# Strassen's scheme in the second layer of a mixture of experts: seven products of quarters for eight

## The chip, the cores and the metric

The kernel runs on one core of a Trainium2 chip. The metric is the device time of one execution in microseconds. Verdicts compare runs of two kernels made on the same chip in the same rounds. Each run has a state; unless one is named as slow below, all runs here are fast ones. The clock below is the one granted to TensorE, as a share of full speed.

## The reference

Attention without a softmax makes 4608 tokens of 512 features. Then a gate gives each token to one of eight experts, in the order of the logits, until each expert has exactly 576. An expert is a two-layer perceptron, all in float32:

```python
N, D, E, F = (4608, 512, 8, 1024)
cap = N // E                                  # 576 tokens per expert
order = np.argsort(-(x @ w_gate).flatten())
for idx in order:                             # greedy, balanced
    tok, e = (int(idx) // E, int(idx) % E)
    if assigned[tok] >= 0 or counts[e] >= cap:
        continue
    assigned[tok] = e
    counts[e] += 1
for e in range(E):
    mask = assigned == e
    h = np.maximum(x[mask] @ w1[e], 0.0)      # 576x512 @ 512x1024
    out[mask] = h @ w2[e]                     # 576x1024 @ 1024x512
```

## The kernel before

The greedy order is not walked. The kernel settles one expert after another, and finds the tokens of each by a search for a threshold. While TensorE computes expert t, the search for the tokens of expert t+1 runs between its matmuls. One step of the search is a round trip: TensorE counts how many tokens lie over each of 32 candidate thresholds (nine small matmuls into `n_ps`), VectorE works out the next candidates in a dozen tiny instructions and one large comparison (`over`), and TensorE loads `over` for the next count.

```python
def compare(over, cand, c0=0, c1=GC):
    nc.vector.tensor_tensor(over[:, c0:c1], ...mx..., ...cand..., op=AL.is_ge)   # 128x1152, both in SBUF

def threshold(t, over):
    for s in range(NSTEP):
        yield (4.6 if t > 1 else 4.3) if s > 0 else ...    # us of matmuls before the next step
        for c in range(0, GC, G):
            nc.tensor.matmul(n_ps, lhsT=over[:, c:c + G]..., rhs=best[:, :, c:c + G], ...)
        # ... need, full, n_full from n_ps
            nc.vector.tensor_scalar(some, in0=n_full..., scalar1=0.5, ..., op0=AL.is_gt)
            nc.vector.transpose(some_t..., some...)
            nc.vector.reduce_sum(out=kk, in_=some_t, axis=AXX)
            nc.vector.tensor_scalar(from_lo, in0=kk, ...)
            for g in range(G):                              # G = 4
                nc.vector.tensor_scalar(ends[g * QP:(g + 1) * QP], in0=from_lo, scalar1=lo_was[0:QP], ...)
        if s + 1 < NSTEP:
            cand_next = candidates(s + 1, lo)
            compare(over, cand_next)
        # ... then assign(): cut, two, sums, ... with both inputs in SBUF
```

The numbers after `yield` are the only timing: a fixed order of TensorE's instructions, in which the next count stands 4.6 us of matmuls after the last. The second layer of an expert takes its 576 tokens as four whole blocks of 128 and a rest of 64:

```python
for n, (a, nr) in enumerate(blocks):
    if nr == P:                                             # a whole block: 8 matmuls of 512 columns
        for f in range(FC):
            nc.tensor.matmul(y_ps, lhsT=hid[:, f, a:a + nr], rhs=w2[:, f, :],
                             start=(f == 0), stop=(f == FC - 1))
            yield 0.858
        nc.scalar.copy(y_sb, y_ps)
    else:
        # ... the rest of 64 rows
    put(t, n, nr, y_sb)                                     # scatter from GpSimd
```

## Time and profile before

| | before |
|---|---|
| time, median of the first 3 runs | 726.95 us (724.67 to 729.97) |
| granted clock, whole run | 0.940 |
| expert stage, eight experts | 534.55 us of the span of 723.6 |
| TensorE idle in the expert stage | 0.87 us (534.55 - 533.68) |
| GpSimd busy in the expert stage | 77.78 us |

First the windows by expert of the kernel before, here the fourth expert, the last one, and the sum of all eight. After the length come the busy us (and instructions) of TensorE, its weight loads, VectorE, ScalarE and GpSimd, then the clock:

```profile
383.40:450.98 67.58, 67.46 (x302) 41.06 (x303) 46.21 (x167) 12.62 (x27) 10.74 (x10) 1.00 0.29 100
651.46:713.75 62.29, 62.24 (x208) 37.34 (x208) 0.68 (x1) 9.51 (x22) 4.80 (x5) 1.00 0.06 19
sum 534.55, PE 533.68 PEld 323.71 DVE 287.42 ACT 98.39 POOL 77.78; mean PE 66.71 PEld 40.46 DVE 35.93 ACT 12.30 POOL 9.72
```

TensorE has almost no idle time, at full clock. The last expert has no search beside it (VectorE is busy for 0.68 us). Second, two lines of the timeline in the middle of a search step, before. A line has the start and the length in us, the engine (PE is TensorE, PEld its weight loads, DVE VectorE, ACT ScalarE, POOL GpSimd), the line of the program (L729), the operation, what it writes and reads, the shapes and the count; a bracket at the end gives the idle time before it and what ended that:

```profile
399.88 5.10 PE L729 MATMUL h_ps<-xt,w_sb 128*128 128x288 f32 x20
401.83 0.92 DVE L500 TENSOR_SCALAR ends<-from_lo,ends 32x2 f32<-32x2 f32 x4
```

### The profile page before, as it was taken

The numbers are of one execution on the slowest core, as the hardware profiler recorded it, in microseconds if no ns is written. First come the engines' busy times: TensorE is split into PE (matmuls) and PEld (weight loads), VectorE is DVE, ScalarE is ACT, GpSimd is POOL, SyncE is SP. The second block draws the span as 40 slices with busy tenths as digits, with TensorE's granted clock in tenths as the row PEclk, the third lists the DMA queues.
The fourth block names the chain that finished last, engine by engine and source line by source line (L and its number), as shares of the span: only waits on it lengthen the run. The fifth ranks groups of instructions, "written<-read, shape, count | busy, mean of one in ns | idle before, by whom it ended". The sixth has DMA issues, their size and how long they took to land.

```text
span 723.6 us, 12335 instructions
## 1 busy us (share of the span) xinstructions
PE 641.3 (89%) x4979; PEld 408.7 (56%) x4979; DVE 395.6 (55%) x1382; ACT 164.5 (23%) x331; POOL 97.5 (13%) x113
## 2 busy tenths in 40 slices
PE   3877788116999999999999999999999999999994
PEld 3666666112764576457546744774576467447641
DVE  4344646888787378657766774887477530010000
ACT  1454555101210311122122202110221122122100
POOL 0100110003004100510041023004100421010011
PEclk9987977557999999999999999999999999999998
DMA  8987898305308200900260054008200944010001
GB/s 286 312 269 262 283 315 322 125 0 194 113 1 298 74 1 3 347 24 0 91 259 23 1 191 173 9 0 295 77 1 10 340 161 169 14 43 8 1 29 36
DMA packets 41400, 93.34 MB, mean 129 GB/s; under 512 B 3456, under 2 KB 3456, under 8 KB 41344
## 3 DMA queue, kind: packets, MB, share of 16 engines
q1 hardware_dynamic: 34752, 72.49, 28.8%
q0 software_dynamic: 5888, 20.06, 7.9%
q8 instruction: 39, 0.64, 0.3%
q14 instruction: 17, 0.14, 0.1%
q10 hardware_dynamic: 704, 0.02, 0.1%
HBM read 72.50 MB, written 20.05 MB: 128 GB/s over the span
## 4 chain that ended last, share of the span: by engine, by line
PE 64%; issue 19%; DVE 9%; DMA 2%; POOL 2%; ACT 2%; POOLq 0%; ACTq 0%; DVEq 0%; SPq 0%
PE y_ps L740 23%; PE h_ps L729 23%; PE o_ps L372 3%; PE qt_ps L303 3%; PE y_ps L750 3%; PE kv_ps L315 3%; DVE over L268 2%; PE t_ps L700 2%; PE n_ps L462 2%; POOL out_dram L709 1%; DMA gw<-in_moe_w_gate_dram 1%; DVE need L468 1%; POOL xg L632 1%; DMA w_sb<-in_moe_w_dram 1%; DVE ends L500 1%
## 5 line engine op out<-in xcount | busy, mean ns | idle before, releaser
L729 PE MATMUL h_ps<-xt,w_sb 128*128 128x288 f32 x1024 | 261.7, 410 | 0.8 <-ACT xt L703 0.8
L740 PE MATMUL y_ps<-w_sb,hid 128*128 128x512 f32 x512 | 227.6, 595 | 0.0
L729 PEld LDWEIGHTS h_ps<-xt,w_sb 128*128 128x128 f32 x1024 | 190.1, 190 | 54.9 <-issue 5.7
L740 PEld LDWEIGHTS y_ps<-w_sb,hid 128*128 128x128 f32 x512 | 94.2, 190 | 100.8 <-issue 100.0
L732 ACT ACTIVATE hid<-h_ps 128x288 f32<-128x288 f32 x128 | 52.6, 411 | 212.4 <-PE h_ps L729 212.4
L709 POOL DMA_INDIRECT out_dram<-y_sb,outs x40 | 44.0, 1101 | 421.1 <-ACT y_sb L745 392.6
L687 DVE TENSOR_TENSOR xs<-xg 128x512 f32<-128x512 f32 (+1 forms) x40 | 27.3, 689 | 75.6 <-PE t_ps L700 65.2
L268 DVE TENSOR_TENSOR over<-mx,cand 128x1152 bf16<-128x1152 f32 (+3 forms) x52 | 67.0, 1288 | 1.6
L757 DVE TENSOR_TENSOR y_sb<-y_ps,y_part 64x512 f32<-64x512 f32 x8 | 5.5, 683 | 105.2 <-ACT y_part L756 105.2
L745 ACT COPY y_sb<-y_ps 128x512 f32<-128x512 f32 x32 | 18.7, 584 | 161.8 <-PE y_ps L740 161.8
L632 POOL DMA_INDIRECT xg<-x_dram,ids x40 | 40.3, 1008 | 76.3 <-DMA w_sb<-in_moe_w_dram 35.9
L703 ACT ACTIVATE xt<-t_ps,g_col 128x512 f32<-128x512 f32 (+1 forms) x40 | 25.8, 645 | 93.5 <-PE t_ps L700 50.6
L462 PEld LDWEIGHTS <-over 128*128 128x128 bf16 x441 | 17.4, 97 | 38.6 <-DVE over L268 30.2
L372 PE MATMUL o_ps<-kvx,qt 64*64 64x72 f32 x1152 | 32.5, 257 | 7.3 <-issue 6.3
L462 PE MATMUL n_ps<-best,over 128*128 128x32 bf16 x441 | 19.4, 179 | 21.0 <-DVE over L268 18.6
L303 PE MATMUL qt_ps<-ident,q_sb 128*128 128x128 f32 x144 | 31.2, 345 | 5.5 <-ACT kvt L336 1.9
L315 PE MATMUL kv_ps<-v_sb,k_sb 64*64 64x64 f32 x1152 | 29.1, 246 | 7.3 <-issue 7.3
L380 DVE TENSOR_REDUCE ms<-sq 128x8 f32<-128x512 f32 x36 | 24.1, 680 | 19.2 <-ACT sq L378 19.0
L372 PEld LDWEIGHTS o_ps<-kvx,qt 64*64 64x64 f32 x1152 | 26.3, 158 | 13.5 <-issue 11.8
L500 DVE TENSOR_SCALAR ends<-from_lo,ends 32x2 f32<-32x2 f32 x144 | 31.6, 219 | 2.8
L700 PEld LDWEIGHTS t_ps<-ident,xs 128*128 128x128 f32 (+1 forms) x160 | 18.3, 140 | 24.3 <-issue 16.7
L315 PEld LDWEIGHTS kv_ps<-v_sb,k_sb 64*64 64x64 f32 x1152 | 26.1, 158 | 8.8 <-issue 8.8
(174 smaller groups left out, 479.0 us busy)
## 6 DMA issues: line engine op xcount, KB each, us to landing
w_sb<-in_moe_w_dram SPq DMA_DIRECT2D x16, 1024.0 KB, 6.2
w_sb<-in_moe_w_dram SPq DMA_DIRECT2D x8, 2048.0 KB, 16.4
k_sb<-in_k_dram SPq DMA_DIRECT2D x16, 576.0 KB, 5.7
v_sb<-in_v_dram SPq DMA_DIRECT2D x16, 576.0 KB, 5.8
q_sb<-in_q_dram SPq DMA_DIRECT2D x16, 576.0 KB, 5.7
x_dram<-o_sb SPq DMA_DIRECT2D x16, 576.0 KB, 4.4
x_dram<-o_sb SPq DMA_DIRECT2D x4, 288.0 KB, 3.4
xg<-x_dram,ids POOLq DMA_INDIRECT x40, 6.5
```

Source lines behind the costliest of these rows:

```text
L268: nc.vector.tensor_tensor(over[:, c0:c1], mx[:, c0:c1].rearrange("p (c o) -> p c o", o=1).to_broadcast([P, c1 - c0, NCAND]), cand[:, 1:NCA ...
L303: nc.tensor.transpose(t_ps[:, x, :], q_sb[:, (4 * n + x) * P:(4 * n + x + 1) * P], ident)
L315: nc.tensor.matmul(kv_ps[cs, l, r * D:(r + 1) * D], lhsT=k_sb[ls, r, j, :], rhs=v_sb[ls, r, j, :], start=(j < 2), stop=(j >= R - 2))
L372: nc.tensor.matmul(o_ps[n * HP:(n + 1) * HP, rp, (2 * r2 + l) * W:(2 * r2 + l + 1) * W], lhsT=turned_q[bn][ks, block // 2, l * HP:(l + 1) ...
L462: nc.tensor.matmul(n_ps, lhsT=over[:, c:c + G].rearrange("p c n -> p (c n)"), rhs=best[:, :, c:c + G], start=(c == 0), stop=(c == GC - G))
L500: nc.vector.tensor_scalar(ends[g * QP:(g + 1) * QP], in0=from_lo, scalar1=lo_was[0:QP], scalar2=None, op0=AL.add)
L632: tokens = nc.gpsimd.indirect_dma_start(out=xg[0:nr].rearrange("p h w -> p (h w)"), out_offset=None, in_=x_dram, in_offset=bass.IndirectOf ...
L700: nc.tensor.transpose(t_ps[:, d, 0:nr], xs[0:nr, d * P:(d + 1) * P], ident[0:nr, 0:nr])
L709: put = nc.gpsimd.indirect_dma_start(out=out, out_offset=bass.IndirectOffsetOnAxis(ap=ids_of[t][0:nr, n:n + 1], axis=0), in_=y_sb[0:nr, :] ...
L729: nc.tensor.matmul(h_ps, lhsT=w1[:, 2 * (d % 2) + d // 2, f * P:(f + 1) * P], rhs=xt[:, d, cs], start=(d == 0), stop=(d == DC - 1))
L732: nc.scalar.activation(hid[:, f, cs], h_ps, ACT.Relu)
L740: nc.tensor.matmul(y_ps, lhsT=hid[:, f, a:a + nr], rhs=w2[:, f, :], start=(f == 0), stop=(f == FC - 1))
```

## The change

Whole blocks hold 512 tokens, so the second layer's 512x1024 by 1024x512 product can be cut in quarters each way. Strassen's scheme (in Winograd's form) makes the result from seven products of quarters instead of eight, and pays with sums of operands before and sums of products after. One eighth of the whole-block second layer is saved on TensorE, which is the bound. The operand sums go to GpSimd, which has most of its time free; results are added on VectorE. Per expert there are on GpSimd four weight differences of 128x1024, eight token sums of 128x512 and one result difference of 128x512; VectorE gets six adds of 128x512.

```diff
+        tw = moe.tile([P, 4, FH, DH], FT, name="tw", tag="tw", bufs=1)
+        t1, t2, t3, t4 = (tw[:, n] for n in range(4))
+        for o, x, y in ((t1, b12, b11), (t2, b22, t1), (t3, b22, b12), (t4, t2, b21)):
+            in_order(nc.gpsimd.tensor_tensor(o, x, y, op=AL.subtract))
 ...
+        def sums(m):
+            ms = slice(m, m + 2)
+            for o, x, y, op in ((s1, a21, a22, AL.add), (s2, s1, a11, AL.subtract), (s3, a11, a21, AL.subtract),
+                                (s4, a12, s2, AL.subtract)):
+                in_order(nc.gpsimd.tensor_tensor(o[:, ms], x[:, ms], y[:, ms], op=op))
 ...
-                for f in range(FC):
-                    nc.tensor.matmul(y_ps, lhsT=hid[:, f, a:a + nr], rhs=w2[:, f, :], ...)
-                    yield 0.858
+        for m, (left, right, then) in enumerate(
+                ((a11, b11, lambda p_ps: nc.scalar.copy(u1, p_ps)), (a12, b21, first_c),
+                 (a22, t4, lambda p_ps: nc.scalar.copy(u5, p_ps)), (s2, t2, lambda p_ps: add(u2, p_ps, u1)),
+                 (s3, t3, seventh), (s1, t1, fifth), (s4, b22, third))):
+            p_ps = psm.tile([P, 2, DH], FT, name="y_ps", tag="y", bufs=3)
+            for n in range(2):
+                for f in range(FH):
+                    nc.tensor.matmul(p_ps[:, n], lhsT=left[:, f, n * P:(n + 1) * P], rhs=right[:, f], ...)
+                    yield 0.4
+            then(p_ps)
```

`in_order` fixes the order of GpSimd's queue. The change also moves the search: as soon as expert t+1's tokens are settled, the search for t+2 begins, still inside expert t, and its VectorE bursts are cut up by pauses. `xt` and `hid`, and in TensorE's result memory (PSUM) the transposes' `t_ps`, get one buffer in place of two to make room.

```diff
         ctl = control(t + 1) ...
+                    if wait is None:
+                        found = True
+                        if t + 2 < E - 1:
+                            ahead = control(t + 2)
+                            wait = next(ahead)
+                elif ahead is not None and used is not None:
+                    wait -= used
+                    if wait <= 0:
+                        wait = next(ahead)
```

## The prediction

The sum came to 727.0 - 25.5 + 11 = 712.5 us, put down as 712. The 11 us for the new wait were the author's guess, under a third of a worst case of 39 us. Rival (a) says that the GpSimd sums don't disturb VectorE, rival (b) that they hold up its search chain in each expert, for which the two stretched instructions spoke, and that the holes may also cost TensorE's clock, which is what its slices show.

> **What bounds the kernel now.** I read the page's busy shares and slices first, then the windows by expert, then the groups of instructions, then the timeline of one expert.
>
> ```profile
> PE 641.3 (89%) x4979; PEld 408.7 (56%) x4979; DVE 395.6 (55%) x1382; ACT 164.5 (23%) x331; POOL 97.5 (13%) x113
> PE   3877788116999999999999999999999999999994
> PEclk9987977557999999999999999999999999999998
> 322.10:389.70 67.60, 67.48 (x303) 41.08 (x303) 46.17 (x167) 12.62 (x26) 10.73 (x10) 1.00 0.28 100
> 592.50:657.00 64.50, 64.50 (x229) 39.30 (x228) 6.38 (x16) 12.62 (x26) 9.72 (x10) 1.00 0.26 93
> ```
>
> From slice 10 on (about 180 us) TensorE is full. The window rows give, after the length, busy us of PE, weight loads, VectorE, ScalarE and GpSimd, then the clock. One inner expert is 67.6 us long, PE has work for 67.48 of them at full clock, VectorE for 46, GpSimd for 11. So in the expert stage (179 to 714 us) every microsecond of matmul removed is a microsecond of time, unless something new makes PE wait.
>
> The last expert has no bookkeeping in it, so its matmuls run undisturbed:
>
> ```profile
> 651.34 31.31 PE L729 MATMUL h_ps<-xt,w_sb 128*128 128x288 f32 x128
> 682.49 27.63 PE L740 MATMUL y_ps<-w_sb,hid 128*128 128x512 f32 x64
> 710.05 3.65 PE L750 MATMUL y_ps<-w_sb,hid 128*64 128x512 f32 x16
> ```
>
> The kernel has 64 first-layer matmuls and 32 whole-block second-layer matmuls per expert, so each f32 matmul is two instructions. Taking off the last one's own length: (31.31 - 0.41)/127 = 0.2433 us per 288-column instruction, (27.63 - 0.59)/63 = 0.4292 us per 512-column one. That is 0.83 ns per column.
>
> Who else is close to setting the pace? The search for the next expert's tokens is a ping-pong between PE and VectorE, laid statically into PE's order:
>
> ```profile
> 400.07 0.15 DVE L468 TENSOR_TENSOR need<-goal,n_ps 32x8 f32<-32x8 f32 x1 [0.75 <-PE n_ps L462]
> ...
> 403.06 1.36 DVE L268 TENSOR_TENSOR over<-mx,cand 128x1152 bf16<-128x1152 f32 x1
> 404.34 0.15 DVE L511 TENSOR_TENSOR ends<-ends 128x1 f32<-128x1 f32 x1
> 404.58 0.52 PEld L462 LDWEIGHTS <-over 128*128 128x128 bf16 x9
> 404.82 0.38 PE L462 MATMUL n_ps<-best,over 128*128 128x32 bf16 x9
> ```
>
> VectorE starts a step at 400.07 and has `over` at 404.42; PE loads it at 404.58. The slack is some 0.2 us, in a step of 5.16 us. Anything that lengthens this chain by more than that stops PE, and PE has no spare time to make it up. This is the weak spot.
>
> [...] Weight loads take 190 ns, less than the 217 ns that a 256-column instruction will need, so I don't expect them to bind. [...] No GpSimd tensor_tensor is in this trace; its only large elementwise work is a one-input 64x512 copy of 0.61 us. [...]
>
> ```profile
> 369.06 1.36 DVE L268 TENSOR_TENSOR over<-mx,cand 128x1152 bf16<-128x1152 f32 x1
> 369.35 1.96 POOL L709 DMA_INDIRECT out_dram<-y_sb,outs  x1 [0.30 <-issue]
> 452.55 0.91 POOL L709 DMA_INDIRECT out_dram<-y_sb,outs  x1 [3.29 <-DVE need L468]
> 453.08 0.37 DVE L492 TENSOR_SCALAR some<-n_full 32x64 f32<-32x64 f32 x1
> ```
>
> The first scatter takes 1.96 us against a median of 0.98: about the time for which `over` still runs. The tiny `some`, normally 0.18 us, takes 0.37 and ends with the GpSimd instruction (453.45 against 453.46). Not every small VectorE instruction beside a GpSimd one is stretched, so the effect is real but its size for a GpSimd tensor_tensor is open.
>
> **The change part by part.**
> Products: 7 of 8 matmuls of 256 columns, 112 instructions, replace 64 of 512 columns. At 0.83 ns per column a 256-column one is 0.2433 - 32 x 0.00083 = 0.2168 us. 112 x 0.2168 = 24.3 us against 64 x 0.4292 = 27.5. Saved: 3.2 us per expert, times 8 = 25.5 us, all on the path. Transposes, search matmuls, first layer and the rest block of 64 rows stay.
> GpSimd: per expert four weight differences of 128x1024, 8 token sums of 128x512 and one result difference of 128x512. [...] Deadlines: the weight differences are first used in product 3, 38 us into the expert; the last sums begin at 31 us and the one used first (the second of four) is due at product 4, about 10 us later. Even behind five gathers (6.5 us) it is there. The first expert's w2 is there in time too: its load takes 16 us and starts with the layer.
> VectorE: six adds of PSUM and SBUF, 128x512. The trace has 0.69 us for such a size (xs), so 4.1 us; it goes from 46 to 50 of some 64 us. ScalarE copies two products in place of four blocks: less. [...] With three PSUM buffers for products of 3.5 us each, PE can run two products ahead of a late add.
> Moved: the search for expert t+2 now starts inside expert t, as soon as t+1's tokens are settled. Walking the generators, its steps still stand 10 first-layer matmuls (4.87 us) or 12 product matmuls (5.2 us) apart, so the slack of one step stays small; the whole search only drifts earlier, and by experts 6 and 7 is out of the way. Weights are fetched earlier, which is harmless. Single buffers for xt, hid and the sums: each is rewritten after its last reader in PE's order, so I see no new wait there.
> End: unchanged in kind, the rest block is still last (copy, add, scatter).
> Sum without new waits: 727.0 - 25.5 = 701.5 us.
>
> **The new wait.** The weight differences start about 2.6 us into an expert (the previous rest block's scatter ends there in the timeline). In experts 1 to 4 they fall on search steps, in expert 5 on the assignment. [...] The best is none. The kernel's many small pauses look like work of someone who timed this on the chip, and who would not have kept a 7 us hole in each expert; the step pause of 4.6 was left as it was. I therefore take about 11 us, under a third of the worst case: 701.5 + 11 = 712.5, which I round to 712.
>
> **The rivals.** (a) [...]the matmul saving comes through whole: 701 to 704. For it: PE is 100% full, the arithmetic is plain, GpSimd and VectorE both have room on average. Against: the scatter of 1.96 us and the 0.2 us of slack. (b) [...]720 to 740, the saving is given back. [...]the slices before 180 us, where PE waits, show 0.5 to 0.7. (c) VectorE's in-order queue: an add delayed behind a search burst holds a product's buffer. Near the end of an expert five scalings (3.4 us), four adds (2.8) and up to two search steps (8.7) fall into about 10 us, which is too much for VectorE; the buffers take some of it. Costs 1 to 2 us per expert, about 8 in all: 710. (d) Weight loads bind at 256 columns: with 0.24 in place of 0.217 us per instruction the saving would be nearly gone (112 x 0.24 = 26.9): about 722. Against: the load is shown as 190 ns and overlaps.
>
> **Range and chances.** 2% is 14.5 us, or 712.4: my centre sits on the border. (a) and (c) fall under or at it, (b) and (d) over it. Range 700 to 730. Faster by over 2%: 0.47. Within 2%: 0.42. Slower: 0.11[...].
>
> **What would show it.** PE's period in the products 0.217 us; the last expert shorter by 3.2 us (62.4 to 59.2) since no search runs in it: that tests the arithmetic alone. In experts 1 to 4: `over`, `ends` or `some` stretched beyond 1.36 and 0.22 us beside GpSimd tensor_tensors, and idle PE before n_ps released by `over`; the sum of these is my 11 us. Product matmuls waiting for a VectorE add would show (c). Wrong would be: an inner expert of 64.4 us with no idle (then 701), or one over 67.6 (then (b)).

## The result, and the profile after

| | before | after |
|---|---|---|
| median of 4 runs | 728.00 us (724.67 to 729.97) | 824.72 us (822.94 to 828.93) |
| granted clock, profiled run | 0.940 | 0.887 |
| sum of the eight experts, counted from 179.20 us | 534.55 us | 632.65 us |
| TensorE busy in them | 533.68 us | 543.51 us |
| TensorE idle in them | 0.87 us | 89.14 us |

The ratio is 1.134 (95% interval 1.128 to 1.141): the changed kernel is slower by 13%. A ratio here is the mean time of one kernel's fast runs over that of the other's fast runs of the same rounds, so it isn't quite the ratio of the medians. The four runs of the changed kernel are fast, and the four before lie within 0.8% of each other.

The page of the changed kernel, its busy shares and two rows of its slices (tenths, 40 slices):

```profile
PE 652.4 (79%) x5362; PEld 501.7 (61%) x5363; DVE 515.6 (63%) x1430; ACT 155.8 (19%) x315; POOL 263.6 (32%) x217
PE   4878871186897698958796988787987996999995
PEclk9978875588997899989898899978998997999998
```

TensorE was full from the eleventh slice on before. Now it has holes nearly everywhere in the expert stage, and its clock is below full in many slices. GpSimd is busy for a third of the span and VectorE for 63%, so by quantity neither is the bound. The windows by expert, for the same fourth expert, the last one and the sum:

```profile
436.52:521.51 84.99, 71.64 (x359) 54.37 (x360) 70.17 (x194) 11.56 (x25) 29.73 (x21) 0.91 0.22 75
752.85:811.85 59.00, 58.95 (x256) 46.45 (x256) 4.74 (x7) 8.34 (x20) 25.36 (x18) 1.00 0.05 18
sum 632.65, PE 543.51 PEld 415.36 DVE 405.38 ACT 89.80 POOL 243.78; mean PE 67.94 PEld 51.92 DVE 50.67 ACT 11.23 POOL 30.47
```

The last expert, with no search in it, got shorter: 62.29 to 59.00 us, 3.29 us saved, with no idle TensorE and full clock, although GpSimd's 25.36 us of work is all there. So the arithmetic works, and the operands are ready in time. The fourth expert, with a search in it, got longer by 17.41 us: TensorE is idle for 13.35 us (84.99 - 71.64) and its clock is 0.91.

What VectorE does meanwhile is the third thing to see: it is "busy" for 70.17 us in place of 46.21. About 4 of these are new adds and some belong to the search that now falls into this expert (without the sums, in the first experiment below, it is 55.97), but the last 14 us are no new work. An instruction that waits for the other engine counts as busy here (`some`, below, with 1.29 us for 0.18). The timeline of the changed kernel in that expert, in a search step from the count on:

```profile
440.93 2.36 POOL L746 TENSOR_TENSOR tw<-w_sb 128x1024 f32<-128x1024 f32 x1
...
442.05 1.29 DVE L492 TENSOR_SCALAR some<-n_full 32x64 f32<-32x64 f32 x1
443.36 2.35 POOL L746 TENSOR_TENSOR tw<-w_sb,tw 128x1024 f32<-128x1024 f32 x1
...
443.89 1.84 DVE L498 TENSOR_SCALAR from_lo<-kk,span 32x2 f32<-32x2 f32 x1
445.67 2.34 POOL L746 TENSOR_TENSOR tw<-w_sb 128x1024 f32<-128x1024 f32 x1
445.77 5.03 DVE L500 TENSOR_SCALAR ends<-from_lo,ends 32x2 f32<-32x2 f32 x4
447.97 2.34 POOL L746 TENSOR_TENSOR tw<-tw,w_sb 128x1024 f32<-128x1024 f32 x1
451.11 1.36 DVE L268 TENSOR_TENSOR over<-mx,cand 128x1152 bf16<-128x1152 f32 x1
452.53 0.42 PE L462 MATMUL n_ps<-best,over 128*128 128x32 bf16 x9 [6.34 <-DVE over L268]
```

Read it in pairs. `some` is issued while the first weight difference runs and ends at 443.34, when that difference has ended (443.29): 1.29 us for 0.18. The second difference starts at 443.36 and `from_lo`, issued at 443.89, ends when it ends: 1.84 us for 0.22. Then the four `ends`: 5.03 us for 0.92, across the third and fourth difference. VectorE gets its turn here about once per GpSimd instruction, and it can miss one: in the kernel with the sums alone (second experiment below) `some` took 2.81 us across a scatter and the first difference. `some_t` and `kk` between them, a transpose and a reduction, keep their lengths (0.23 and 0.21 us) beside the second difference. The step takes 11.67 us from count to count (440.86 to 452.53) where it took 5.17. TensorE has matmuls for 5.1 us of that, and the bracket of the last line says the rest: 6.34 us idle until `over` was there. The list of waits of the changed kernel, in the expert stage alone, sums such holes up (total us, times, longest):

```profile
PE n_ps L462 <- DVE over L268: 56.8, 14, 9.1
PE a_ps L617 <- DVE along L614: 12.3, 2, 7.1
PE all_ps L529 <- DVE sums_b L525: 10.5, 2, 8.0
PE t_ps L715 <- DVE xs L701: 9.3, 5, 2.7
```

Together they are 88.9 of the 89.14 us of idle time. `along` and `sums_b` belong to the assignment that follows a search, `xs` are the scaled tokens. The kernel before has no wait for `over` listed in this stage; its 18.6 us of them lie ahead of it.

### The profile page after: what moved, and what is told of

Same layout as the page of the kernel before. It is cut to its first block, busy times and chain, and to the rows that moved or that the text cites. A ratio compares the mean times of both kernels' runs of the same rounds, so it can differ in the third digit from the quotient of the medians.

```text
span 821.7 us, 13270 instructions
## 1 busy us (share of the span) xinstructions
PE 652.4 (79%) x5362; PEld 501.7 (61%) x5363; DVE 515.6 (63%) x1430; ACT 155.8 (19%) x315; POOL 263.6 (32%) x217
## 5 line engine op out<-in xcount | busy, mean ns | idle before, releaser
L765 PE MATMUL h_ps<-xt,w_sb 128*128 128x288 f32 x1024 | 280.4, 434 | 0.8 <-ACT xt L718 0.8
L756 POOL TENSOR_TENSOR sh<-hid 128x512 f32<-128x512 f32 x32 | 42.7, 1336 | 148.6 <-ACT hid L768 148.6
L814 PE MATMUL y_ps<-tw,sh 128*128 128x256 f32 x384 | 90.3, 390 | 0.0
L462 PE MATMUL n_ps<-best,over 128*128 128x32 bf16 x441 | 19.7, 181 | 77.2 <-DVE over L268 75.4
L814 PEld LDWEIGHTS y_ps<-tw,sh 128*128 128x128 f32 x384 | 73.3, 194 | 9.7
L785 DVE TENSOR_TENSOR y_sb<-y_ps,u 128x512 f32<-128x512 f32 x24 | 16.4, 684 | 92.2 <-PE y_ps L814 92.2
L500 DVE TENSOR_SCALAR ends<-from_lo,ends 32x2 f32<-32x2 f32 x144 | 63.9, 443 | 2.8
L814 PE MATMUL y_ps<-w_sb,hid 128*128 128x256 f32 x256 | 60.5, 392 | 0.0
L814 PEld LDWEIGHTS y_ps<-w_sb,hid 128*128 128x128 f32 x256 | 49.7, 196 | 7.4
L746 POOL TENSOR_TENSOR tw<-w_sb 128x1024 f32<-128x1024 f32 x16 | 37.6, 2351 | 12.2 <-DMA w_sb<-in_moe_w_dram 12.0
L814 PE MATMUL y_ps<-w_sb,sh 128*128 128x256 f32 x128 | 35.2, 410 | 0.0
```

What stands on the lines that cost most here:

```text
L462: nc.tensor.matmul(n_ps, lhsT=over[:, c:c + G].rearrange("p c n -> p (c n)"), rhs=best[:, :, c:c + G], start=(c == 0), stop=(c == GC - G))
L746: in_order(nc.gpsimd.tensor_tensor(o, x, y, op=AL.subtract))
L756: in_order(nc.gpsimd.tensor_tensor(o[:, ms], x[:, ms], y[:, ms], op=op))
L765: nc.tensor.matmul(h_ps, lhsT=w1[:, 2 * (d % 2) + d // 2, f * P:(f + 1) * P], rhs=xt[:, d, cs], start=(d == 0), stop=(d == DC - 1))
L814: nc.tensor.matmul(p_ps[:, n], lhsT=left[:, f, n * P:(n + 1) * P], rhs=right[:, f], start=(f == 0), stop=(f == FH - 1))
```

## The experiments

My theory after reading the trace: (T1) the operand sums on GpSimd hold up VectorE's search chain, instruction by instruction; TensorE idles, and its clock drops with the longer holes (it is 0.50 from 452.5 to 455 us, after the hole of 6.34 us above). This is theory L of the expectations. The rivals: (T2) the moved search or the split VectorE work stretch the chain by themselves; (T3) Strassen's products don't come through at full rate (weight loads, buffers, adds on VectorE).

### Both halves apart

The first experiment keeps everything of the change but the sums: the products read unsummed quarters (and give a wrong result).

```diff
-        for o, x, y in ((t1, b12, b11), (t2, b22, t1), (t3, b22, b12), (t4, t2, b21)):
-            in_order(nc.gpsimd.tensor_tensor(o, x, y, op=AL.subtract))
+        t1, t2, t3, t4 = b11, b22, b12, b21
+        s1, s2, s3, s4 = a21, a22, a11, a12
...
-            in_order(nc.gpsimd.tensor_tensor(quarter(1, 0), u3, u5, op=AL.subtract))
+            nc.scalar.copy(quarter(1, 0), u3)
```

> The changed kernel with all operand sums and the result difference on GpSimd taken out; the products read unsummed quarters, so the result is wrong on purpose. All else stays: seven products, six VectorE adds, the search moved ahead. Theory L [...]: nearly the whole loss goes, 702 to 715 us, clock in the expert stage back to 0.98 or more, `ends` back at 0.22 us. Rival V (VectorE's extra adds and the moved search overload it): the loss stays, 780 us or more. Rival N (256-column matmuls cost more than their columns): the last expert stays above 60 us.

Measured: 731.83 us (725.11 to 733.92), ratio 1.006 (0.999 to 1.014). Against the changed kernel's 1.134 the sums alone are worth 0.128 of about 727, or 93 us: most of the loss. But the time is not the 702 to 715 expected. The windows of this kernel, the fourth and the last expert:

```profile
399.42:468.58 69.16, 64.58 (x359) 50.36 (x360) 55.97 (x198) 12.18 (x26) 8.21 (x9) 1.00 0.27 94
663.25:722.25 59.00, 58.90 (x256) 46.41 (x256) 4.74 (x7) 8.95 (x21) 4.80 (x5) 1.00 0.05 18
```

TensorE has 64.58 us of work, 2.9 less than before, and the expert is 1.6 us longer all the same. The saving of 8 x 3.29 = 26.3 us is there and some 31 us are lost elsewhere (26.3 + 0.006 x 727). That is T2 or part of T3, and is taken up below.

The second experiment is the reverse: the kernel before, with its old second layer and its old search, and the same 13 GpSimd instructions per expert at the same places, whose results nobody reads (right result).

```diff
+        for o, x, y in ((t1, b12, b11), (t2, b22, t1), (t3, b22, b12), (t4, t2, b21)):
+            in_order(nc.gpsimd.tensor_tensor(o, x, y, op=AL.subtract))
...
+                if c == 1 and f in units[3::4]:
+                    sums(f % FH - 1)
...
+                if n == 2:
+                    in_order(nc.gpsimd.tensor_tensor(s1[:, 0:2], a11[:, 0:2], a12[:, 0:2], op=AL.subtract))
```

> The kernel before (ordinary second layer, search where it was) with only the 13 GpSimd tensor_tensors per expert added at the same points of the program, on the same operands, results unused (the result stays right). Theory L: GpSimd's own 20 us per expert are beside the path, yet the time rises by some 100 us, to 800 to 860 us; `ends`, `from_lo` and `some` stretched to about one GpSimd instruction each. Rival V: no VectorE work was added, so 725 to 740 us.

Measured: 850.59 us (848.5 to 854.75), ratio 1.172 (1.166 to 1.179). TensorE's and VectorE's programs are those of the kernel before, apart from the order of the hidden units and single buffers for `xt` and `hid`; nobody waits for the sums; and they cost 126 us. The last expert, where the sums meet no search, stays at 62.29 us, so neither the order nor the buffers matter there. So the loss doesn't come from late operands. An inner expert of this kernel:

```profile
352.11:440.17 88.06, 73.55 (x302) 43.82 (x303) 63.56 (x167) 12.60 (x27) 31.54 (x23) 0.90 0.21 77
```

It has the 302 matmuls of the kernel before, and TensorE is busy with them for 73.55 us in place of 67.46. That is the clock, in the same kernel's windows around a hole of 8.3 us (the clock is the number after the five engines):

```profile
358.00:362.00 4.00, 0.00 (x0) 0.00 (x0) 3.95 (x3) 0.00 (x0) 4.00 (x3) 1.00 0.00 0
362.00:366.20 4.20, 0.00 (x1) 0.01 (x1) 4.10 (x6) 0.00 (x0) 1.98 (x1) 0.53 0.00 0
366.20:369.50 3.30, 3.30 (x16) 2.51 (x17) 2.50 (x15) 0.41 (x1) 0.00 (x0) 0.56 0.02 5
369.50:372.50 3.00, 3.00 (x14) 2.34 (x13) 1.54 (x3) 0.52 (x2) 0.00 (x0) 1.00 0.00 0
```

TensorE stops at about 357.9. The clock stays full for the first 4 us of the hole, is half in the rest of it, and still half for about 2.9 us after work begins again at 366.2. This hole costs its own length and then again a little. The two other holes of this expert, of 3.20 and 3.02 us, are followed by half clock too: 0.50 from 386.5 to 389.5 us, and 0.50 from 408 to 412 us.

### The clock by itself

If the lower clock is a second cost on top of the holes, filling the holes with useless matmuls must gain time, although it adds work to the full engine. In the kernel with the sums alone, 28, 10 and 10 useless bf16 matmuls were put ahead of the three longest holes of an expert.

```diff
+            if t > 1 and s in (1, 4):
+                warm(28 if s == 1 else 10)
...
+        assigned.append(0)
+        if len(assigned) > 2:
+            warm(10)
```

> The kernel before with the GpSimd sums (e2), plus useless bf16 matmuls put into PE's order just ahead of the three places per expert where PE stands still longest: 28 ahead of the second search step (6.0 us in a hole of 8.3), 10 ahead of the fifth and 10 ahead of the assignment (2.2 us in holes of 3.0 to 3.2), for experts 2 to 6. If the clock falls because PE stands still, more work makes it faster: some 5 us less per expert, 25 us in all, 820 to 832 us against 850. If the low clock has another cause, the same or slower: 848 us or more.

Measured: 826.44 us (821.7 to 828.97), ratio 1.134 (1.130 to 1.139), 24 us less than without the filler (850.59; by the two ratios 28, since the kernel before took 2.5 us more in this set). The same inner expert as above, now:

```profile
348.45:430.81 82.36, 78.01 (x347) 45.60 (x351) 63.66 (x167) 12.61 (x26) 31.59 (x23) 1.00 0.24 82
```

The clock is back at 1.00 and the expert is 5.7 us shorter with more matmuls in it. The clock's share of the loss of this kernel is thus some 6 us per inner expert, and the rest is the holes themselves.

### Which instructions hold up the chain, and why

Is it the reading of SBUF or any GpSimd instruction at all? In the kernel with the sums alone, memsets of equal length, which only write, took their place (2.36 and 1.26 us on average).

```diff
-            in_order(nc.gpsimd.tensor_tensor(o, x, y, op=AL.subtract))
+            in_order(nc.gpsimd.memset(tw.rearrange("p a f d -> p (a f d)")[:, 0:2700], 0.0))
...
-                in_order(nc.gpsimd.tensor_tensor(o[:, ms], x[:, ms], y[:, ms], op=op))
+                filled = nc.gpsimd.memset(sh.rearrange("p a f d -> p (a f d)")[:, 0:1400], 0.0)
```

> The kernel before with GpSimd memsets in place of the 13 sums[...]: they write SBUF and read nothing. If GpSimd's reads are what collides, 727 to 735 us. [...] 770 to 850 us.

Measured in two runs: 832.44 us (828.16 and 836.72), ratio 1.148 (1.139 to 1.157). That is in the second of the two ranges, which stood for writes that hold up the chain as well: writing alone does most of the damage (0.148 of 0.172). The timeline of this kernel where four memsets meet the end of a search:

```profile
395.03 4.25 DVE L500 TENSOR_SCALAR ends<-from_lo,ends 32x2 f32<-32x2 f32 x4
395.35 5.23 POOL L749 MEMSET sh<- 128x1400 f32 x4 [16.20 <-ACT hid L767]
399.51 0.23 DVE L517 TENSOR_TENSOR cut<-mx,ends 128x72 bf16<-128x72 f32 x1
```

Four `ends` of one input take 4.25 us for 0.92, beside memsets. But `cut`, which reads two SBUF operands, runs beside the last memset in 0.23 us, its normal time; in the changed kernel, beside a weight difference that reads SBUF, the same `cut` took 2.33. So the two kinds of instruction differ in these runs: `ends` is held up beside GpSimd instructions that read (5.03 us for four) and beside ones that only write (4.25 us), `cut` beside one that reads (2.33 us) and not beside one that writes (0.23 us). The reduction `kk` takes 0.21 us on average in the kernel before, in the changed one and in this one. `over`, with two inputs and 1.36 us long, passes a memset unharmed as well: here it lies within the second of three and keeps its length (the mean of all 48 is 1.36 us in this run), where beside token sums of the changed kernel it took 2.30 and 2.37 us.

```profile
181.11 7.18 POOL L740 MEMSET tw<- 128x2700 f32 x3
183.56 1.36 DVE L268 TENSOR_TENSOR over<-mx,cand 128x1152 bf16<-128x1152 f32 x1
```

One case doesn't fit plainly: a `mid` with two inputs took 1.24 us for 0.30 beside a memset. It stood right behind a cast that waited for the same memset (`sums_b`, 1.32 us for 0.17), and whether it waited by itself can't be told from the trace.

The length of one GpSimd instruction should set the wait if VectorE's turn comes once per instruction. The same sums in pieces of 256 elements (34 per expert in place of 13):

```diff
-            in_order(nc.gpsimd.tensor_tensor(o, x, y, op=AL.subtract))
+            for f in range(FH):
+                in_order(nc.gpsimd.tensor_tensor(o[:, f], x[:, f], y[:, f], op=AL.subtract))
```

> The kernel before with the same GpSimd sums, cut into instructions of 256 elements (0.6 us instead of 2.35 and 1.27; 34 instead of 13 per expert). Theory L[...]: single waits shrink to about 0.6 us, but there are more of them, so the time stays high, 800 to 860 us. If long single holds are the trouble, small pieces would cure it: 760 us or less.

Measured: 793.09 us in the fast run (a second run, 805.67, counts as slow, being 1.6% longer, so there is no interval). That is just under the expected 800: better than whole sums by 57 us, though GpSimd is busier. An inner expert takes 78.5 us instead of 88.1:

```profile
416.96:495.45 78.49, 70.29 (x302) 42.47 (x303) 60.82 (x167) 12.62 (x26) 36.82 (x44) 0.96 0.25 86
```

A piece took 0.72 to 0.84 us on average, not the 0.6 expected, so GpSimd works 5 us longer than with whole sums, and yet the loss over 67.6 is half. That fits turns that come oftener and cost less each; it speaks for T1 and against any explanation by GpSimd's total.

How much is due to each kind of sum? The kernel with the sums alone, with only the four weight differences left:

```diff
                 if c == 1 and f in units[3::4]:
-                    sums(f % FH - 1)
+                    pass
```

> The kernel before with only the four weight differences per expert on GpSimd (9.4 us, 2.35 us each), without the token sums. In e2 they make the 8.3 us hole and 1.7 us of low clock in each of some six experts: 10 us times 6 = 60 us, so 780 to 795 us, about half of e2's loss; the rest is the token sums'.

Measured: 796.51 us (792.0 to 798.28), ratio 1.096 (1.092 to 1.100), a microsecond and a half over what I expected. The four differences cost about 70 us and the other nine sums about 55 (0.076 of 727), though these last are shorter each. Eight of the nine come in two bursts of four, some 5.1 us each. In the trace of the second experiment the three bursts of the inner expert shown above make these three holes:

```profile
366.20 0.42 PE L462 MATMUL n_ps<-best,over 128*128 128x32 bf16 x9 [8.29 <-DVE over L268]
386.37 0.42 PE L462 MATMUL n_ps<-best,over 128*128 128x32 bf16 x9 [3.20 <-DVE over L268]
407.41 0.20 PE L529 MATMUL all_ps<-sums_b,ones_b 128*128 128x16 bf16 x1 [3.02 <-DVE sums_b L525]
```

The first is that of the differences, the others are those of the token sums. Together they are the whole idle time of that expert (88.06 - 73.55 = 14.51 us). All four differences fall into one step of the search: from `need` to the end of `over` it takes 12.71 us for 4.35, so 9.37 us of GpSimd work delay it by 8.36. A burst of sums delays a step by 3.70 us (8.05 for 4.35) with 5.06 us of work.

The obvious remedy is VectorE itself: the changed kernel with all sums on VectorE at the same places.

```diff
-            in_order(nc.gpsimd.tensor_tensor(o, x, y, op=AL.subtract))
+            nc.vector.tensor_tensor(o, x, y, op=AL.subtract)
```

(three such places).

> The changed kernel with every operand sum and the result difference issued on VectorE at the same place in the program (result right). VectorE gets some 10 us more work per expert and runs it in one piece of 5 us in front of the search, but nothing can alternate with GpSimd. Theory L: far better than the changed kernel though VectorE does more: 735 to 775 us. Rival V (VectorE's amount of work sets the time): worse than the changed kernel, 830 us or more.

Measured: 788.09 us (787.4 to 790.4), ratio 1.088 (1.082 to 1.094). That is over the range, so VectorE is no place for them beside a search, but it is 37 us better than GpSimd (34 by the two ratios). In the last expert, where nothing disturbs, the 13 sums add 20.56 us to GpSimd (25.36 in the changed kernel against 4.80 without sums) and 10.50 us to VectorE (15.24 against 4.74). The chain is held up either way; VectorE is done in half the time.

### What the arrangement costs

To see what the moved search does alone, the changed kernel got its ordinary second layer back, with no sums and no adds.

```diff
-        turns = {(6, 1), (6, 3), (6, 5), (6, 7)} if t == 0 else {(5, 4), (5, 7), (6, 2), (6, 5)}
-        for m, (left, right, then) in enumerate(
 ...
+        for n, (a, nr) in enumerate(blocks[0:NB - 1]):
+            for f in range(FC):
+                nc.tensor.matmul(y_ps, lhsT=hid[:, f, a:a + nr], rhs=w2[:, f, :], ...)
+                yield 0.858
+            nc.scalar.copy(y_sb, y_ps)
+            put(t, n, nr, y_sb)
```

> The changed kernel with the ordinary second layer (eight products' worth, no GpSimd sums, no VectorE adds), but the search moved ahead with its new pauses and the single buffers. Theory L: nearly the time before, 725 to 740 us; a hole of about 2.4 us where the moved search starts right after the last choice (the changed kernel's trace shows one with no GpSimd tensor_tensor beside it) would give up to 12 us. Rival V: the moved search itself costs much, 770 us or more.

Measured: 743.77 us (741.0 to 744.74), ratio 1.025 (1.019 to 1.031), a few us over the range. The moved search loses 19 us with no Strassen near: the first expert takes 75.8 us for 69.0, and the fourth and fifth 73 for 67.6. In the expert stage TensorE is idle for 13.4 us: 7.8 in 3 places for `over`, where there was no such wait before, and 5.2 in 3 for `xs`. The other 5.8 us are matmuls that ran longer (539.54 us busy for 533.71).

The reverse, Strassen's products and adds without sums but with the old schedule of the search (wrong result):

```diff
-        ahead = None
         for t in range(E):
-            ctl, more = ahead, t + 1 < E
-            if ctl is None and more:
-                ctl = control(t + 1)
-                wait = next(ctl, None)
+            ctl = control(t + 1) if t + 1 < E else iter(())
+            wait = next(ctl, None)
 ...
```

> The run without sums, with the search put back where the kernel before has it: what remains of the change is seven products and VectorE's six adds (result wrong on purpose). The move alone cost 19 us in the last set; if the parts add up, 731.8 - 19.1 = 713 us. If the adds cost nothing beside the search, 724.7 - 25.5 = 699 us; if the cost in the run without sums came from the adds and not from the move, 720 us or more.

Measured: 724.35 us (718.4 to 726.18), ratio 0.997 (0.990 to 1.003). I expected 713, so this failed too: it lies in the range of the third case, 720 us or more. The move is not all that eats the saving. An inner expert takes 68.2 us with 64.6 of TensorE work, 3.6 us idle. The waits shown are for `t_ps`, the transposes of the next expert's tokens, which come in the last two products: 10.6 us in 7 places wait for `xs` and 7.0 us in 5 for `xt`. So I put the transposes later, only within the last product:

```diff
-        turns = {(6, 1), (6, 3), (6, 5), (6, 7)} if t == 0 else {(5, 4), (5, 7), (6, 2), (6, 5)}
+        turns = {(6, 1), (6, 3), (6, 5), (6, 7)}
```

> The run with products and adds only and the search unmoved (e5), with one thing changed: the transposes for the next expert stand after matmuls 1, 3, 5 and 7 of the last product instead of from the middle of the last but one. In e5 the inner experts had 64.6 us of PE work but took 68.2, and PE's waits there were for a scaled block (2.2 us) and for the single transpose buffer (1.3 us). If the place of the transposes is the cause, not the six adds themselves: inner experts of 64.6 to 66 us and 703 to 710 us in all. If VectorE is simply overloaded by the adds: 718 us or more. Result wrong on purpose (no sums).

Measured: 721.23 us (719.04 to 722.89, 6 runs), ratio 0.992 (0.989 to 0.994). That lies in the second range: most of the time lost is not the place of the transposes. The waits for `t_ps` are gone from the head of the list, but TensorE has a new wait in the same stretch:

```profile
370.98 1.36 DVE L268 TENSOR_TENSOR over<-mx,cand 128x1152 bf16<-128x1152 f32 x1
372.25 1.29 DVE L698 TENSOR_TENSOR xs<-xg 128x512 f32<-128x512 f32 x2
373.46 1.48 DVE L776 TENSOR_TENSOR u<-y_ps,u 128x512 f32<-128x512 f32 x2
...
374.20 1.13 PE L805 MATMUL y_ps<-w_sb,hid 128*128 128x256 f32 x4 [2.07 <-DVE u L776]
```

VectorE works almost without a break from 363.0 to 373.5 on the assignment of one expert's tokens, the set-up of the next search and two scalings, and the add that should free a product's buffer stands behind it in the queue. TensorE needs that buffer and waits 2.07 us, here and five times more (11.4 us in 6 places). The clock takes the rest: TensorE's idle time in the expert stage fell from 19.7 us in the previous experiment to 12.6, but its busy time rose by 6.2. After this hole, which ended at 374.20, the clock falls to 0.64 in the second us and 0.50 in the third:

```profile
374.00:375.00 1.00, 0.80 (x4) 0.73 (x5) 0.83 (x2) 0.03 (x1) 0.00 (x0) 1.00 0.00 0
375.00:376.00 1.00, 1.00 (x7) 0.92 (x6) 0.96 (x2) 0.59 (x1) 0.00 (x0) 0.64 0.00 0
376.00:377.00 1.00, 1.00 (x4) 0.82 (x4) 0.93 (x2) 0.69 (x1) 0.47 (x1) 0.50 0.00 0
```

In the changed kernel no such wait is listed: its earlier search with pauses keeps VectorE free for these adds, which looks like the reason for it. But that costs 19 us by itself. Either way 20 to 31 us are lost against the 26.3 gained, even with operand sums for nothing.

### A version that gains

What remains is to use the scheme where no search runs: in the last two experts. They get Strassen's products with the sums on VectorE, which is idle there; the first six experts keep the old second layer, and the search its old schedule (right result).

```diff
+        fast = t >= E - 2
...
+            if fast and c == 1 and f == units[2]:
+                differences()
+            if fast and c == 1 and f in units[3::4]:
+                sums(f % FH - 1)
+        for n, (a, nr) in enumerate(() if fast else blocks[0:NB - 1]):
+            # ... the ordinary second layer
+        for m, (left, right, then) in enumerate(() if not fast else
+            # ... the seven products
```

> A version meant to beat both: the search where it was, ordinary second layer in the first six experts, the seven products only in the last two, where no search runs, with the sums on VectorE, idle there. Result right. The last expert was 3.2 to 3.3 us shorter in every run of the seven products; two of them: 724.7 - 6.5 = 718 us, 717 to 720, about 0.9% faster. If VectorE's 15 us of sums and adds don't fit in, no gain.

Measured: 721.37 us (714.83 to 723.04, 6 runs) against 725.87 for the kernel before in the same rounds, ratio 0.992 (0.988 to 0.997): 0.8% faster, a little over the time expected. By the measure of 2% that counts as the same time, but the interval lies under 1. Both experts gained their 3.3 us, to compare with 65.32 and 62.29 before:

```profile
590.36:652.38 62.02, 61.81 (x284) 48.54 (x285) 23.71 (x48) 11.56 (x24) 9.71 (x10) 1.00 0.31 107
652.38:711.38 59.00, 58.95 (x256) 46.46 (x256) 15.23 (x20) 8.33 (x20) 5.53 (x5) 1.00 0.05 18
```

Counted from the first matmul of the expert stage (183.38 us here, 179.17 before), its eight experts took 528.0 us for 534.6, which is twice 3.29; the stage ahead of it ended between 175.8 and 184.1 us in the traces of all runs, so the total varies by more than this gain. It is the best of the kernels with a right result, and beats both the kernel before and the changed one.

## Why the prediction was wrong

It said 712 us, 700 to 730, and gave "slower" 0.11. The time was 824.72.

- **Where the bound is: right.** TensorE was full, and the chain of the search with its 0.2 us of slack was the weak spot.
- **The saving: right.** It was 25.5 us from 3.2 per expert; the last expert measured 3.29, so 26.3. The last expert was predicted at 59.2 and took 59.00. Rival (d), weight loads that bind at 256 columns, is refuted by that: nearly its whole saving would have gone.
- **The lengths on GpSimd: right within a tenth in sum.** The trace of the changed kernel shows 2.35 us for a weight difference and, for the token sums, 1.34 on average, their own waits included. Thirteen sums took 20.6 us in the last expert, where nothing disturbs.
- **The new wait: this is the step that failed.** "I therefore take about 11 us, under a third of the worst case", which was 39 us. The sums cost 93 us in the changed kernel. Four things were wrong in that term. First, the differences: I spread a burst over two or three steps and took off the gaps of each. It falls into one step, and in the kernel with the sums alone it makes a hole of 8.29 us. Second, the token sums: I counted them in some six places in all, but they come in two bursts of four in each expert, which make holes of 3.20 and 3.02 us there. So an inner expert loses 14.5 us and the six experts that have a search beside them some 83 together, where the worst case was 39 and I took 11; in the changed kernel all idle time is 89.14 us. Third, the clock: I named it in rival (b), but put no microseconds to it. In the kernel with the sums alone it costs about 6 us per inner expert. Fourth, I cut the result to under a third because a careful author "would not have kept a 7 us hole in each expert". That is an argument about a person, not about the machine; the profile had just shown me a chain with 0.2 us to spare.
- **Rival (b)**, the search chain held up in each expert, was the nearest, at 720 to 740 too small for the same reasons. **Rival (c)**, VectorE's queue holding a product's buffer, was named with "about 8 in all". With the old search it is 11.4 us of waits; in the changed kernel none is listed. The prediction said of the move that "the whole search only drifts earlier": it costs 19 us, which is the second, smaller miss.

The windows above begin at 179.20 us in both kernels, but the first matmul of the expert stage lies at 179.17 us before and at 177.45 in the changed kernel. From there, for all eight experts:

```profile
179.17:713.75 534.58, 533.71 (x2257) 323.75 (x2257) 287.45 (x1033) 98.39 (x205) 77.78 (x74) 1.00 0.27 94
177.45:811.85 634.40, 545.26 (x2641) 416.79 (x2641) 407.10 (x1080) 89.80 (x189) 243.78 (x178) 0.92 0.23 79
```

The sum then reads: they got longer by 99.8 us. Of it -26.3 are the arithmetic, +88.3 more idle TensorE (89.14 - 0.87), and the remaining +37.8 are matmuls that ran longer: TensorE was busy 545.26 us where 533.71 - 26.3 = 507.4 would do. That this last part is the clock is shown for the sums alone, by 73.55 against 67.46 us of the same 302 matmuls and by the filler; for the changed kernel I infer it from the clock of 0.92. It isn't quite all of it: products and adds alone, at full clock (1.00 in each expert), are busy for 510.30 us, 2.9 more than 507.4.

What stays open: how the 19 us of the moved search divide between its pauses and its single buffers, which no run took apart, and which of its pauses could be chosen better.

## What to carry to other kernels

Before elementwise work goes to GpSimd because GpSimd is idle, look for a chain of small VectorE instructions that runs at the same time with TensorE waiting at its end. Each of them may be held up for most of a GpSimd instruction (here, beside differences of 2.35 us, `some` took 1.29 us for 0.18 and `from_lo` 1.84 for 0.22), so add up the GpSimd bursts that meet the chain, take off only the gaps of the chain, and add the clock that TensorE loses after some of the holes (here the clock fell to 0.50 after one of 2.07 us, and in the first experiment it stayed at 1.00 over the expert with one of 3.02 us); busy shares show none of it, and VectorE's own busy time hides it. A saving on the bound engine is best placed first where no such chain runs, and measured there: here that is two experts of eight, and 0.8%.
